# An attention recurrence with an MLP behind it: all 4630 entries of the order relisted

## The chip, the cores and the metric

The kernel runs on one core of one Trainium2 chip. A core has a matrix engine (TensorE, called PE in the profile, with its weight loads as PEld), a vector engine (VectorE, DVE), a scalar engine (ScalarE, ACT), a general engine (GpSimd, POOL) and an engine that here only issues DMAs (SyncE, SP). Each engine takes its own instructions in the order in which the program lists them, and waits at an instruction until what it needs is there. The metric is the device time of one execution in microseconds; less is better.

## What is computed

The first part is a linear attention with a state, 4 batches times 8 heads, 768 steps, 40 dimensions a head:

```python
for t in range(S):
    kt, vt, rt = (k[:, :, t], v[:, :, t], r[:, :, t])
    wt, at, bt = (w[:, :, t], a[:, :, t], b[:, :, t])
    y[:, :, t] = np.einsum('bhd,bhde->bhe', rt, state)
    Sa = np.einsum('bhde,bhe->bhd', state, at)
    state_decay = state * wt[:, :, None, :] - np.einsum('bhd,bhe->bhde', Sa, bt)
    state = state_decay + np.einsum('bhd,bhe->bhde', vt, kt)
```

Its result y, as a matrix x of 3072 tokens by 320, goes through an MLP with 2048 hidden columns:

```python
h = x @ w_in
sp = np.maximum(h, 0.0) + np.log1p(np.exp(-np.abs(h)))
g = h * erf(sp)
return (g @ w_out).astype(np.float32)
```

The weights w_in and w_out come in float64; all else is float32.

## The kernel before

**Staging.** The recurrence is cut into chunks of 32 steps. Four chunks are one segment, and there are 12 segments: two groups of batches, six segments each, and so 48 chunks one after the other, since the state MT is passed from each to the next. The MLP takes the 256 tokens of a finished segment at a time (128 steps of two batches). So the MLP of segment q lies beside the recurrence of the segments behind q, and the first MLP product can only start when the four chunks of segment 0 are through.

**Preparing a segment** has three steps that don't need the state. `prep` loads w, checks it on ACT (L447) and forms running products of it with scans on DVE (L439 and L443, two instructions each, a reciprocal L449 between them). `aphase` runs once for each chunk: it loads k, b and a, scales them on DVE (L472 makes Ab, L477 makes bk), multiplies them on PE (L482, the A product, in bank pA), masks the result on DVE (L489, two instructions), stores a part of it to DRAM, and transposes bk on PE (L500, also in pA). `tphase` runs once for a segment: it reads the parts back as Ti, inverts small triangular blocks by a recursion of 14 steps of two small DVE instructions (L529 and L530), stores the result to DRAM (TD), reads it back in another layout (Tb), transposes it on DVE (L538), and forms the rest of the inverses by two groups of small products on PE (L547, the W group and the DAD group, 64 products each, which the profile counts twice, as 128), with a copy between them and a sum (L554) behind.

**The chain of a chunk** (`chain`) is what passes the state on: copies of MT into Zm, product Z (L593), copy zt, product U (L602), copy Us, transpositions (L618, L627), product PQ (L636) and its mask on DVE (L639, into Vu), product MY (L647, L651), and then two DVE instructions that both read the bank my: L654 adds to MT, and L658 makes the output y in Pr. Behind the last chunk of a segment four transfers store y to DRAM.

**The weights** are unpacked on DVE from the words of the float64 numbers, by three instructions for each 512 columns (L737, L738, L739); those of w_in also need two split operations on PE (L754, L755) and copies of the low part (wlo). All this lies in the first 100 us.

**The MLP.** `load_x` reads y back and splits it into xh and xl. A layer-1 operation (`mm1`, L823) is eight products that split float32 into parts; two of them fill a bank ph of 128 x 512. There are 192 such operations. A copy moves ph to h (L375 when ACT does it, L377 when DVE does). `unit` takes four such blocks through six activations on ACT (L831) and two instructions on DVE (L856, L857). `post` finishes a block with L868 and L869 on DVE and four layer-2 operations on PE (L878); there are 384 of those.

**What sets the order.** `Plan.add` collects 4630 operations with what they read and write. `schedule` then gives each operation its engine by one letter of the table `ENGINES` (P for PE, A for ACT, V for DVE, G for POOL, S for SP), and `emission` writes the operations out in the sequence of the table `ORDER`, which is a list of the numbers 0 to 4629. The place in that list is all that decides what stands behind what on an engine:

```python
for i in order:
    o = N.P.ops[i]
    N.cur = i
    o["fn"](o["eng"])
```

Waits between engines follow from what the operations read and write. SP issues all the transfers, in the order of the list too. `start` also adds 190 dummy products on PE (`warm`, L422), whose result nothing reads; the list puts them where PE would else be idle, and all stand ahead of the second layer-1 block.

Of the kernel before, what the change touches and what calls it, by code (L numbers as in the profile page):

```python
# [1008 lines left out]
```

## Time and profile before

| what | value |
|---|---|
| time, median of 3 runs | 762.17 us (760.15 to 765.23) |
| span of the profiled execution | 754.8 us |
| PE busy | 722.7 us (96%) |
| DVE busy | 643.1 us (85%) |
| ACT busy | 573.3 us (76%) |
| POOL busy | 5.6 us (1%) |
| mean granted TensorE clock | 0.991 of full speed |
| DMA, mean over the span | 125 GB/s |
| largest PE groups: layer 2 (L878), layer 1 (L823, five forms) | 265.2 us, 376.2 us |

The span is the time from the first to the last instruction of one profiled execution; the device time of the runs also has what lies around it. Busy times are those of one engine, and an average over the whole span: the kernel has a start in which the MLP can't run yet, a long middle, and a short end, and these have to be looked at apart. The dummy products count as busy time of PE.

### The profile page before, as it was taken

How to read it: one execution, taken by the hardware profiler on the slowest of the kernel's cores; microseconds unless marked ns; L12 is line 12 of the kernel's file. 1: busy time of each engine (PE TensorE's matmuls, PEld its weight loads, DVE VectorE, ACT ScalarE, POOL GpSimd, SP SyncE). 2: the span in 40 equal slices, each digit the busy share in tenths (PEclk: the TensorE clock that was granted, in tenths of full speed). 3: DMA queues.
4: the chain of work that ended last, by engine and by line, in shares of the span. 5: the costliest groups of instructions: out<-in, count | busy, mean ns of one | idle time of the engine just before them, and what ended most of it. 6: DMA issues, size and time to landing. Idle time of an engine off the chain costs nothing.

```text
span 754.8 us, 32087 instructions
## 1 busy us (share of the span) xinstructions
PE 722.7 (96%) x13807; PEld 570.4 (76%) x13807; DVE 643.1 (85%) x1461; ACT 573.3 (76%) x1122; POOL 5.6 (1%) x15
## 2 busy tenths in 40 slices
PE   9968899789999999999999999999999999999996
PEld 3645558668778778878878888887888787888874
DVE  8887878889879899998889899998997898878774
ACT  3322544987988998888898897898988888776992
POOL 2000000000000000000000000000000000000000
PEclk9988999999999999999999999999999999999999
DMA  8687566655564655555545556546545444312000
GB/s 255 175 256 197 142 160 153 144 124 122 129 147 121 131 140 126 118 125 126 131 126 136 132 134 139 130 104 138 140 103 115 124 112 92 104 41 61 21 17 22
DMA packets 165616, 94.63 MB, mean 125 GB/s; under 512 B 115452, under 2 KB 148988, under 8 KB 165468
## 3 DMA queue, kind: packets, MB, share of 16 engines
q1 hardware_dynamic: 165468, 92.51, 50.1%
q8 instruction: 110, 1.80, 1.1%
q14 instruction: 38, 0.31, 0.1%
HBM read 73.48 MB, written 14.16 MB: 116 GB/s over the span
## 4 chain that ended last, share of the span: by engine, by line
PE 83%; ACT 5%; DVE 5%; DMA 3%; issue 2%; SPq 1%; DVEq 0%
PE po L878 29%; PE ph L823 22%; PE my L647 4%; PE ph L422 4%; PE pA L547 4%; PE pQ L636 4%; PE pA L482 3%; PE my L602 2%; PE my L593 2%; PE pA L500 2%; PE pQ L618 2%; PE my L651 2%; SPq L381 1%; PE pQ L627 1%; ACT l L831 1%
## 5 line engine op out<-in xcount | busy, mean ns | idle before, releaser
L878 PE MATMUL po<-wo,h 128*128 128x320 f32 x768 | 265.2, 454 | 1.1 <-DVE h L869 1.1
L878 PEld LDWEIGHTS po<-wo,h 128*128 128x128 f32 x768 | 125.5, 189 | 30.5 <-DVE h L869 1.9
L831 ACT ACTIVATE l<-l 128x512 f32<-128x512 f32 x192 | 111.0, 624 | 8.3 <-DVE nd L856 7.5
L823 PE MATMUL ph<-xh,wih 128*128 128x256 f32 x384 | 113.8, 378 | 0.0
L823 PEld LDWEIGHTS ph<-xh,wih 128*128 128x128 f32 x384 | 69.5, 190 | 24.1 <-issue 0.3
L823 PE MATMUL ph<-xh,wil 128*128 128x256 f32 x384 | 77.2, 282 | 0.7 <-issue 0.7
L823 PE MATMUL ph<-xl,wih 128*128 128x256 f32 x384 | 76.9, 282 | 0.0
L856 DVE TENSOR_TENSOR nd<-l,r 128x512 f32<-128x512 f32 x96 | 64.3, 687 | 9.6 <-ACT r L831 8.4
L868 DVE TENSOR_TENSOR l<-l,r 128x512 f32<-128x512 f32 x96 | 64.5, 682 | 1.2 <-ACT l L831 0.4
L869 DVE SCALAR_TENSOR_TENSOR h<-l,h 128x512 f32<-128x512 f32 x96 | 64.6, 684 | 0.5
L857 DVE SCALAR_TENSOR_TENSOR r<-nd,r 128x512 f32<-128x512 f32 x96 | 64.2, 683 | 0.2
L831 ACT ACTIVATE l<-h 128x512 f32<-128x512 f32 x96 | 57.6, 627 | 4.2 <-DVE h L377 3.1
L823 PEld LDWEIGHTS ph<-xh,wil 128*128 128x128 f32 x384 | 59.5, 190 | 0.7 <-issue 0.7
L375 ACT COPY h<-ph 128x512 f32<-128x512 f32 x84 | 48.9, 583 | 14.2 <-PE ph L823 13.4
L823 PEld LDWEIGHTS ph<-xl,wih 128*128 128x128 f32 x384 | 59.2, 189 | 0.0
L831 ACT ACTIVATE r<-r 128x512 f32<-128x512 f32 x96 | 55.3, 623 | 0.4
L831 ACT ACTIVATE r<-l 128x512 f32<-128x512 f32 x96 | 54.9, 621 | 0.3
L422 PE MATMUL ph<-d 104*128 104x512 bf16 x190 | 53.3, 401 | 1.6 <-DVE d L392 1.6
L823 PE MATMUL ph<-xl,wir 128*128 128x256 f32 x192 | 54.2, 282 | 0.0
L823 PE MATMUL ph<-xh,wir 128*128 128x256 f32 x192 | 54.1, 282 | 0.0
L375 ACT COPY Zm<-MT 40x320 f32<-40x320 f32 x62 | 28.3, 457 | 28.7 <-DVE MT L654 24.1
L489 DVE TENSOR_TENSOR Zs<-pA,tri 64x256 f32<-64x256 f32 x96 | 40.6, 423 | 11.1 <-PE pA L482 6.0
(142 smaller groups left out, 1346.4 us busy)
## 6 DMA issues: line engine op xcount, KB each, us to landing
bk<-in_kba_e SPq DMA_DIRECT2D x46, 416.0 KB
vt<-in_rv_e SPq DMA_DIRECT2D x96, 120.0 KB
wo<-in_moe_w_in SPq DMA_DIRECT2D x10, 512.0 KB
h<-in_moe_w_out SPq DMA_DIRECT2D x10, 512.0 KB
Pr<-in_w_e SPq DMA_DIRECT2D x12, 419.7 KB
Rt<-in_r_e SPq DMA_DIRECT2D x48, 104.0 KB
Vu<-in_v_x SPq DMA_DIRECT2D x96, 40.0 KB
Zm<-in_v_s SPq DMA_DIRECT2D x48, 80.0 KB
```

The costliest lines, as they stand in the source:

```text
L375: self.nc.scalar.copy(o, i)
L422: P.add("warm", "PE", lambda e: nc.tensor.matmul(s.ph[1], s.d1[:, :128], s.d1[:, :512], start=True, stop=True), ["d1"], ["phw"], -1e3, 0.22)
L489: P.add("Am", "DVE", lambda e, x=x, xs=xs: nc.vector.tensor_tensor(out=zx[64:128, x], in0=pz[xs], in1=s.tri[xs, None, :].to_broadcast([64, ...
L547: nc.tensor.matmul(pw[js, i, ts], l[js, i], r[js, i, ts], start=True, stop=True)
L636: nc.tensor.matmul(pq[i % 2 * 64:i % 2 * 64 + 64, i // 4, i // 2 % 2], vr[:, 256 + n_ * 64:320 + n_ * 64], vr.rearrange("p (a x) -> p a x" ...
L823: nc.tensor.matmul(ph[:, j * 256:j * 256 + 256], a[:k, fs], b[:k], start=(m == 0), stop=(m == 7))
L831: self.P.add(name, "ACT", lambda e: nc.scalar.activation(out=o, in_=i, **kw), rd, wr + ["act"], pr, 0.62)
L856: P.add("nd", [("DVE", 0.69)], lambda e, r=r, l=l, nd=nd: s.eng(e).tensor_tensor(out=nd, in0=l, in1=r, op=ALU.mult), [("l", il), ("r", ir) ...
L857: P.add("rho", "DVE", lambda e, r=r, nd=nd: nc.vector.scalar_tensor_tensor(out=r, in0=nd, scalar=2 * C4, in1=r, op0=ALU.add, op1=ALU.mult) ...
L868: P.add("E", [("DVE", 0.69)], lambda e: s.eng(e).tensor_tensor(out=l, in0=l, in1=r, op=ALU.mult), [("r", ir)], [("l", il)], pr)
L869: P.add("G", "DVE", lambda e: nc.vector.scalar_tensor_tensor(out=h, in0=l, scalar=-1.0, in1=h, op0=ALU.add, op1=ALU.mult), [("l", il)], [( ...
L878: nc.tensor.matmul(po, h[:, bs], s.wo[:, f], start=(f == 0), stop=(f == 15))
```

## The change

The tables `ORDER` and `ENGINES` are replaced. No other line differs: the same 4630 operations, with the same reads and writes. The new table is written in more lines, so every line behind it has a number that is 30 higher (L489 becomes L519, L823 becomes L853). In `ENGINES`, DVE goes from 1421 operations to 1443, ACT from 1109 to 1086, SP from 822 to 826, POOL from 11 to 8; PE keeps its 1267. The first line of the table as it was and as it is (the dummies have the numbers 27 to 216):

```diff
 ORDER = tuple(int(x) for x in """
-6 10 2 3 27 28 29 30 31 32 33 34 35 36 37 38 39 40 41 42 43 44 45 46 47 48 49 50 51 52 53 54 55 56 57 58 59 60 61 62 25 63 64 65 66 67 15 23 518 68 69 70 71 72 73 74 75 76 77 78 79
...
+2 3 23 6 17 14 16 7 4 15 11 8 19 26 10 21 20 518 5 27 28 29 30 31 32 33 34 35 36 37 38 39 40 41 42 43 44 45 46 47 48 49 50 51 52 53 54 55 56 57 58 59
...
```

Three places show what the lists do. A row is a line, an operation, its output and its inputs, and the shape; numbers behind a name are those of its buffer.

**DVE, the first microseconds, from the scans of segment 0 to the first Ab.** In the names wo and h are here the raw words of the weights, Wt and Pr the running products. Before:

```order
L738 SCALAR_TENSOR_TENSOR r_139<-wo,r_139 128x512
L739 SCALAR_TENSOR_TENSOR l_132<-wo,r_139 128x512
L737 TENSOR_SCALAR r_140<-wo 128x512
L377 COPY Zm_77<-MT 40x8x40
L738 SCALAR_TENSOR_TENSOR r_142<-wo,r_142 128x512
L449 RECIPROCAL d_115<-Wt_86 104x8
L443 SCALAR_TENSOR_TENSOR Pr_87<-Pr_87,d_115 104x516 x2
L444 COPY Pr_87<-Wt_86 104x8
L737 TENSOR_SCALAR r_139<-wo 128x512
L738 SCALAR_TENSOR_TENSOR r_139<-wo,r_139 128x512
L739 SCALAR_TENSOR_TENSOR l_136<-wo,r_139 128x512
L472 TENSOR_TENSOR Ab_76<-bk_99,Pr_87 104x512
```

Now:

```order
L469 SCALAR_TENSOR_TENSOR Wt_86<-Pr_87,d_114 104x516
L469 SCALAR_TENSOR_TENSOR Wt_86<-Pr_87,d_114 104x517
L479 RECIPROCAL d_115<-Wt_86 104x8
L473 SCALAR_TENSOR_TENSOR Pr_87<-Pr_87,d_115 104x516 x2
L474 COPY Pr_87<-Wt_86 104x8
L502 TENSOR_TENSOR Ab_76<-bk_99,Pr_87 104x512
L507 TENSOR_TENSOR bk_99<-bk_99,Wt_86 104x512
L407 COPY Zm_77<-MT 40x8x40
L767 TENSOR_SCALAR r_139<-wo 128x512
L767 TENSOR_SCALAR r_140<-wo 128x512
L768 SCALAR_TENSOR_TENSOR r_140<-wo,r_140 128x512
```

The scans, Ab and bk of the first chunk now stand at the front, and the unpacking of the weights behind them. The scan instruction is listed as SCALAR_TENSOR_TENSOR here; the trace calls it TENSOR_TENSOR_SCAN.

**PE, the W and DAD groups of segment 2.** po and wo are the bank and the weights of layer 2, my and pQ banks of the chain, pA the bank that W, DAD and A share. Before:

```order
L618 MATMUL pQ<-ident,MT 104x104 x4
L593 MATMUL my<-Zm_77,Zs_68 32x40 x16
L878 MATMUL po_165<-wo,h 128x320
L547 MATMUL pA<-T_106,Ap 32x16 x64
L878 MATMUL po_164<-wo,h 128x320 x2
L547 MATMUL pA<-Tb_83,W_104 32x16 x64
L878 MATMUL po_165<-wo,h 128x320
L482 MATMUL pA<-Ab_76,bk_99 64x2x32 x8
L602 MATMUL my<-zt_110,Tb_83 32x40 x16
```

Now:

```order
L577 MATMUL pA<-T_106,Ap 32x16 x16
L908 MATMUL po_164<-wo,h 128x320
L908 MATMUL po_165<-wo,h 128x320
L648 MATMUL pQ<-ident,MT 104x104 x4
L908 MATMUL po_165<-wo,h 128x320 x2
L577 MATMUL pA<-T_106,Ap 32x16 x48
L623 MATMUL my<-Zm_77,Zs_68 32x40 x16
L908 MATMUL po_165<-wo,h 128x320
L908 MATMUL po_164<-wo,h 128x320 x2
L908 MATMUL po_165<-wo,h 128x320
L577 MATMUL pA<-Tb_83,W_104 32x16 x64
L908 MATMUL po_164<-wo,h 128x320
```

Between the two groups of 64 there were two layer-2 products, and now there are a Z product and four layer-2 products; the first group is in two pieces.

**DVE, the end of segment 0's last chunk.** r, wo and h belong to the unpacking of the weights, vt, Vu, MT and Pr to the chain; the second L658 and the L654 beside it are the last chunk's. Before:

```order
L529 TENSOR_TENSOR tmp_107<-Ti 128x14
L530 TENSOR_TENSOR Ti<-Ti,tmp_107 128x14
L738 SCALAR_TENSOR_TENSOR r_139<-h,r_139 128x512
L658 TENSOR_TENSOR Pr_87<-my,Pr_87 104x8x32
L737 TENSOR_SCALAR r_141<-h 128x512
L472 TENSOR_TENSOR Ab_76<-bk_99,Pr_89 104x512
L639 TENSOR_TENSOR Vu_79<-pQ,tri 128x8x32
L477 TENSOR_TENSOR bk_99<-bk_99,Wt_86 104x512
L739 SCALAR_TENSOR_TENSOR wo<-h,r_139 128x512
L654 TENSOR_TENSOR MT<-MT,my 104x4x2x40
L658 TENSOR_TENSOR Pr_87<-my,Pr_87 104x8x32
L584 TENSOR_TENSOR MT<-MT,Pr_88 104x4x2x40
```

Now:

```order
L559 TENSOR_TENSOR tmp_107<-Ti 128x14
L560 TENSOR_TENSOR Ti<-Ti,tmp_107 128x14
L407 COPY vt_109<-pQ 104x8x32
L642 COPY Vu_79<-Us_85 32x4x40
L669 TENSOR_TENSOR Vu_79<-pQ,tri 128x8x32
L688 TENSOR_TENSOR Pr_87<-my,Pr_87 104x8x32
L507 TENSOR_TENSOR bk_99<-bk_99,Wt_86 104x512
L502 TENSOR_TENSOR Ab_76<-bk_99,Pr_89 104x512
L688 TENSOR_TENSOR Pr_87<-my,Pr_87 104x8x32
L684 TENSOR_TENSOR MT<-MT,my 104x4x2x40
L767 TENSOR_SCALAR r_141<-h 128x512
L614 TENSOR_TENSOR MT<-MT,Pr_88 104x4x2x40
```

L639 (now L669) has come ahead of the L472 (now L502) of the next segment, two small copies that ACT did stand ahead of it on DVE, and the last L658 (now L688) stands ahead of the L654 (now L684) of the same chunk.

## Rows read from the trace of the kernel before

**Rows 1.** Windows: stretch, length, busy of PE, PEld, DVE, ACT, POOL, PEclk, DMA, GB/s.
```profile
0.00:61.00 61.00, 51.07 (x292) 29.80 (x293) 50.65 (x110) 17.82 (x40) 5.62 (x15) 0.92 0.81 223
61.00:115.80 54.80, 49.51 (x1341) 31.02 (x1340) 43.09 (x103) 22.27 (x59) 0.00 (x0) 0.99 0.64 164
115.80:250.00 134.20, 126.33 (x2766) 105.97 (x2768) 116.83 (x277) 111.83 (x227) 0.00 (x0) 1.00 0.57 136
250.00:700.00 450.00, 447.77 (x9171) 366.14 (x9171) 397.23 (x916) 381.17 (x734) 0.00 (x0) 1.00 0.50 118
700.00:754.80 54.80, 48.01 (x248) 37.48 (x246) 35.28 (x59) 40.25 (x64) 0.00 (x0) 0.97 0.04 14
```

**Rows 2.** Windows of line L422 alone: stretch, length, PE, PEld, PEclk, DMA, GB/s.
```profile
0.00:116.00 116.00, 52.91 (x189) 18.09 (x189) 0.96 0.73 196
```

**Rows 3.** Timeline of PE: start us, length us, engine, line, out<-in, count [idle before, releaser].
```profile
1.62 21.34 PE L422 MATMUL ph<-d 104*128 104x512 bf16 x85 [1.62 <-DVE d L392]
23.97 0.69 PE L482 MATMUL pA<-Ab,bk 104*64 104x64 f32 x16
...
69.36 0.57 PE L500 MATMUL pA<-ident,bk 104*128 104x104 f32 x4 [0.47 <-DVE Zs L489]
...
115.83 0.48 PE L823 MATMUL ph<-xh,wih 128*128 128x256 f32 x2
```

**Rows 4.** Timeline of DVE, the same columns.
```profile
12.84 2.36 DVE L443 TENSOR_TENSOR_SCAN Pr<-Pr,d 104x516 f32<-104x516 f32 x2
...
19.37 0.69 DVE L477 TENSOR_TENSOR bk<-bk,Wt 104x512 f32<-104x512 f32 x1
24.76 0.86 DVE L489 TENSOR_TENSOR Zs<-pA,tri 64x256 f32<-64x256 f32 x2 [2.29 <-issue]
...
36.12 0.88 DVE L489 TENSOR_TENSOR Zs<-pA,tri 64x256 f32<-64x256 f32 x2 [0.38 <-issue]
...
43.63 0.17 DVE L529 TENSOR_TENSOR tmp<-Ti 128x14 f32<-128x14 f32 x1
...
50.21 0.19 DVE L530 TENSOR_TENSOR Ti<-Ti,tmp 128x14 f32<-128x14 f32 x1
...
53.34 1.29 DVE L739 SCALAR_TENSOR_TENSOR l<-wo,r 128x512 int32<-128x512 int32 x2
...
60.95 0.71 DVE L538 STREAM_TRANSPOSE T<-Tb 128x512 f32<-128x512 f32 x1 [1.02 <-DMA Tb<-TD]
...
101.11 0.69 DVE L472 TENSOR_TENSOR Ab<-bk,Pr 104x512 f32<-104x512 f32 x1 [1.32 <-DMA Zs<-Ab]
...
103.35 0.49 DVE L654 TENSOR_TENSOR MT<-MT,my 104x320 f32<-104x320 f32 x1
```

**Rows 5.** The chain that ended last, in order of time: start us, length us, what.
```profile
22.96 0.43 PE po L754 x2
...
51.02 4.67 DMA TD<-Ti
...
56.45 4.38 DMA Tb<-TD
...
163.44 1.30 issue
...
215.26 1.33 issue
...
655.37 0.73 PE po L878 x2
...
720.40 0.54 PE po L878 x2
```

**Rows 6.** Groups by line: engine, operation, shape, count | busy us, mean ns | idle before.
```profile
L375 ACT COPY h<-ph 128x512 f32<-128x512 f32 x84 | 48.9, 583 | 14.2 <-PE ph L823 13.4
L377 DVE COPY h<-ph 128x512 f32<-128x512 f32 x12 | 8.1, 685 | 5.6 <-PE ph L823 4.4 <-PE po L878 1.2
```

**Rows 7.** Timeline of ACT, the columns of rows 3.
```profile
4.93 1.06 ACT L447 ACTIVATE Pr<-Pr 104x1024 f32<-104x1024 f32 x1 [0.97 <-DMA Pr<-in_w_e]
```

More of the change, by code (lines that the diff above doesn't have):

```diff
@@ new lines @@
+VVVVVSSSSVPPPPAPPPPVSVVVAPVPASVVVAPVPASVVVAPAPVSVVVAPAPVSVVVAPAPASVVVAPAPASVVVAPAPASVVVAPAPASVVVAAAPAAPAASVVVAAAPVAPAASVVVSVVVSVVVSVVVSVVVSVVVSVVVSVVV
+SVVVSVVVSAVVAVSVSSVPVVSSPVSVSSVPVVSSPVSVSSVPVVSSPASVSSVPVVSSPASSSSSSVVPAPAVVAAPAPAPVPVVSSSSSSAAPAPAAAAVPAPAPVPVVSSSSSSVAPAPAAAAAPVPAPVPVVSSSSSSAAPAPAV
+AAAPAPVPVPVVSSSSSSSSAAVVVVVVVVVVVVVVVVVVVVVVVVVVVVSSSSVPPPPAPPPPVSAVSAVSSAVPPAAPPAAPPVAPPVAAAAAAAAAAAAAAAVVVVVVVVAAAAAPPAAPPAAPPVAVVPPPPPPAAVVPPPPVVPP
+PPVVPPPPSAVVAVSVSSVPVVSSPASVSSVPVVSSPASVSSVPVVSSPVSVSSVPVVSSPASSSSSSVAVPAPAAVAVPAPAPVPVVSSSSSSVAPAPASAAAPAPVPVPVVSSSSSSVVPAPASAASPVPAPVPVVSSSSSSAAPAPA
@@ new lines @@
+VAASPVPVPVPVVSSSSSSSSAAVVVVVVVVVVVVVVVVVVVVVVVVVVVVSSSSVPPPPVPPPPVSAVSVVSSAVAAAAAAAAAAAAAAVVVVVVVVAAAAAPPAAPPAAPPAAVVPPPPPPAAVVPPPPVVPPPPVVPPPPASASAAA
+AAAAAAAAAAAVVVVVVVVAAAAAPPAAPPAAPPAAVVPPPPPPAAVVPPPPVVPPPPVVPPPPSAVVVVSVSSVPVVSSPASVSSVPVVSSPASVSSVPVVSSPASVSSVPVVSSPVSSSSSSVVVPAPAAAAVPAPAPVPVVSSSSSS
+AAPAPAAVSAPAPAPVPVVSSSSSSVAPAPAASVAPAPVPVPVVSSSSSSAAPAPVAVAAPAPVPVPVVSSSSSSSSAAVVVVVVVVVVVVVVVVVVVVVVVVVVVVSSSSVPPPPAPPPPVSAVSAVSSVVAAAAAAAAAAAAAAVVVV
+VVVVAAAAAPPAAPPAAPPAAVVPPPPPPAAVVPPPPVVPPPPVVPPPPASASAAAAAAAAAAAAAAVVVVVVVVAAAAAPPAAPPAAPPAAVVPPPPPPAAVVPPPPVVPPPPVVPPPPSAVVVVSVSSVPVVSSPASVSSVPVVSSPA
@@ new lines @@
+SVSSVPVVSSPASVSSVPVVSSPASSSSSSVVAPAPAVSVVPVPAPVPVVSSSSSSVAPAPAASAAPVPAPVPVVSSSSSSAAPAPASSSVPAPAPVPVVSSSSSSVAPAPAVAVVPAPAPVPVVSSSSSSSSAAVVVVVVVVVVVVVVV
+VVVVVVVVVVVVVSSSSVPPPPVPPPPVSVVSVVSSVVAAAAAAAAAAAAAAVVVVVVVVAAAAAPPAAPPAAPPAAVVPPPPPPAAVVPPPPVVPPPPVVPPPPASVSAAAAAAAAAAAAAAVVVVVVVVAAAAAPPAAPPAAPPAAVV
+PPPPPPAAVVPPPPVVPPPPVVPPPPSAVVAVSVSSVPVVSSPASVSSVPVVSSPASVSSVPVVSSPASVSSVPVVSSPASSSSSSVAAPVPVSAVVPAPVPVPVVSSSSSSAAPAPASASAPAPAPVPVVSSSSSSAAPAPAASAVPAP
+VPVPVVSSSSSSAVPAPVAVSVPAPVPVPVVSSSSSSSSAAVVVVVVVVVVVVVVVVVVVVVVVVVVVVSSSSVPPPPVPPPPVSVVSAVSSVVAAAAAAAAAAAAAAVVVVVVVVAAAAAPPAAPPAAPPAAVVPPPPPPAAVVPPPPV
@@ new lines @@
+VPPPPVVPPPPASVSAAAAAAAAAAAAAAVVVVVVVVAAAAAPPAAPPVAPPAAVVPPPPPPAAVVPPPPVVPPPPVVPPPPSAVVVVSVSSVPVVSSPASVSSVPVVSSPASVSSVPVVSSPASVSSVPVVSSPASSSSSSVAAPVPAA
+ASVPAPVPVPVVSSSSSSVAPAPAASVAPAPAPVPVVSSSSSSAAPAPASSAAPAPVPVPVVSSSSSSAAPAPVAAVAPAPAPVPVVSSSSSSSSAAVVVVVVVVVVVVVVVVVVVVVVVVVVVVSSSSVPPPPAPPPPVSAVSAVSSAV
+AAAAAAAAAAAAAAVVVVVVVVAAAAAPPAAPPAAPPAAVVPPPPPPAAVVPPPPVVPPPPVVPPPPASASAAAAAAAAAAAAAAVVVVVVVVAAAAAPPAAPPAAPPVAVVPPPPPPAAVVPPPPVVPPPPVVPPPPSAVVAVSVSSVP
+VVSSPASVSSVPVVSSPASVSSVPVVSSPASVSSVPVVSSPVSSSSSSVAVPVPVVVVVPVPAPVPVVSSSSSSAAPAPVAVASPAPAPVPVVSSSSSSAAPAPASSVSPAPAPVPVVSSSSSSAAPVPVAASAPAPAPVPVVSSSSSSS
```

41 lines of the change are left out of this document (15 added, 26 removed), and 269 rows, old and new, of the table ORDER.

## The prediction

> **What bounds the kernel now.** I read the busy times by stage first [rows 1]. The columns to compare are the length of a stretch and PE's busy time in it. From 250 to 700 us PE is idle for 450.00 - 447.77 = 2.2 us in all, although DVE (88%) and ACT (85%) are nearly as full. A new order of the same operations can hardly save anything there. From 115.8 to 250 us PE is idle for 7.9 us. From 700 us to the end it is idle for 6.8 us, most of it behind the last product, which no order hides. Up to 115.8 us PE looks 87% busy, but 52.9 us of that are dummy matmuls of L422 [rows 2]. So the kernel has two halves. Up to the first layer-1 matmul at 115.83 us [rows 3] nothing but a chain of latencies counts. Behind it PE works through a fixed list. The end moves with the moment at which that list can start, and with the 7.9 us of holes just behind it.
>
> Next I followed the chain of latencies on PE [rows 3], on DVE [rows 4] and through the transfers [rows 5]: first A product at 23.97 us, last masked A block (L489) from 36.12 to 37.00, recursion (L529, L530) from 43.63 to 50.40, two transfers through DRAM (TD, Tb), transposition L538 at 60.95, then four chunks that each end with L654 (the last at 103.35), the store and reload of x, and the first matmul of the MLP at 115.83. The reader is to see that the first A waited behind 85 dummies and the split operation after them. Its last input, L477 at 19.37, was done at about 20.0, and DVE then stood idle for 2.29 us ahead of its first L489.
>
> **The change, part by part.** No operation is added or taken away; the tables decide order and engine alone. Counted over both tables, DVE gains 22 operations and ACT loses 23. By their durations in the profile that is about 9 us moved from ACT to DVE, spread over the run: net eight copies of ph (583 ns on ACT, 685 on DVE [rows 6]), six of vt, five of the output and some smaller ones.
>
> *First chunk.* Before, nine weight operations (L737, L738, L739) stand ahead of the first L472; after, none. The scans need w, which had landed when ACT checked it at 4.93 us [rows 7]. From there two scan pairs at 2.36, a reciprocal and a copy (0.4), L472 and L477 at 0.61 (two weight operations in a row take 1.29, so one more of this size costs 0.61 [rows 4]): done at 11.3 us. PE now has 38 dummies ahead of the first A instead of 86: 1.62 + 38 x 0.251 (85 took 21.34 [rows 3]) = 11.2 us. So the first A runs at 11.3 us, 12.7 earlier. Little of this is passed on, for the dummies are only moved. Between the first and the second A there are now 35 of them (8.8 us), three split operations of 0.86 (two steps of 0.43 [rows 5]) and a transposition, so the second A runs at 24.2 us; by the same count the third at 27.4, the fourth at 31.2, and the last L489 ends at 32.4 instead of 37.0: **4.6 us** earlier.
>
> *Recursion.* Behind the last L489 DVE has 7.9 us of work before the recursion (four weight operations, two scan pairs, a copy) where it took 6.6. Start at 40.3 instead of 43.63, end at 47.1 instead of 50.40: **3.3 us**.
>
> *The two transfers.* From the recursion's end to L538 it took 10.55 us, of which TD 4.67 and Tb 4.38 [rows 5], with the DMA engines at 0.81 over the first 61 us [rows 1]. The bulk loads are the same in either order, and five of the w_out loads are issued ahead of Tb in both. The gain is 3.3 us if the trip takes as long as it did. If it is shorter, DVE's own list between recursion and transposition (8.0 us of it) is the bound, and the gain is 5.8. I take **4.0**, near the row, since the loads are only pressed into a shorter time. The Trainium skill (DMA: Bandwidth & Descriptors, section Latency and other measured facts) gives a DMA a fixed cost of about 2 us, mostly HBM latency that rises with load; with two trips of about that, DVE's list would be the bound and the whole sum 753.9 us. The trace's 4.67 and 4.38 speak against it while bulk loads run beside.
>
> *To the first U.* Before, a transposition (L500) that waited 0.47 us for DVE [rows 3] stood ahead of the first U (L602); now it stands behind. Against that, six split operations stand ahead of the W products instead of partly between them. **0.8 us** gained (0 to 1.5).
>
> *The chunks.* Before, L639 of the last chunk stood behind an L472 that waited 1.32 us for a transfer [rows 4] and took 0.61; now L639 comes first, but behind two small copies (0.6). In the chunk before, 0.9 us of small copies and a recursion step are put ahead of L639. Net **0.6 us** gained (between 0.9 lost and 1.8 gained). In the last chunk L658, which the store of x waits for, is put ahead of L654: **0.4 us**.
>
> So the first layer-1 matmul comes 4.0 + 0.8 + 0.6 + 0.4 = 5.8 us earlier, at 110.0 us (bounds 2.4 and 9.5).
>
> *Behind it.* PE has the same 192 layer-1 and 384 layer-2 operations. A layer-2 operation takes 0.54 us behind a full-width one and 0.73 behind a group of narrow tiles [rows 5], so grouping could save time. But the steps from narrow to full width, counted in PE's two lists, are 176 in each. That is worth nothing. What does change is the spacing of the W and DAD groups (L547; each product is short, and 128 of them stand in a group). Before, 1.3 us of other work lies between them in segment 2 and 2.4 in segment 3, and PE stood still inside the second group for 1.30 and 1.33 us with nothing to wait for that the profile shows [rows 5]. After, 2.8 and 5.0 us lie between; in segment 5 it shrinks from 3.3 to 1.2. I take **1.5 us** gained, between 0 and the 2.6 of these two rows.
>
> The price: between the first layer-1 and the first layer-2 operation DVE's list grows by 2.7 us (two L856, one L857, one L868 and one copy of ph more, some small copies fewer). DVE is 87% busy from 115.8 to 250 us [rows 1], so some of it shows: **0.8 us** lost (0 to 2.7). ACT's list there keeps its length.
>
> Sum: 5.8 + 1.5 - 0.8 = 6.5 us. The profiled execution has a span of 754.8 us; the median of the runs is 762.17, so about 7.3 us lie around the span if that execution was a middling one. Predicted: 748.3 us of span, **755.7 us** of time.
>
> **Rivals.** *The start gives more.* The transfers land early, the chunks close up, the stalls go: at most 9.5 + 2.6 = 12.1 us. Half-way from the forecast to that is 9.5 us, a time of 752.7. For it: by the lists alone, with no transfer late, the first layer-1 matmul could come at 107.6. Against it: some thirty waits must all be met.
>
> *The gain is eaten.* TD and Tb are held by the bulk loads, the holes behind 115.8 us stay and DVE's longer list shows: 2.4 - 0.8 = 1.6 us gained, time about 760.6. For it: the DMA engines are at 0.81 already. A page's rule goes the same way for one term: by the Trainium skill (Runtime: NRT & Kernel Launch, section Instruction fetch mechanics) the refill of an engine's instruction memory is mostly hidden, so the stalls at L547 would have another cause, which spacing need not cure; that alone would give 757.2. The two rows without a releaser show a stall, not its cause.
>
> *Slower.* DVE becomes what PE waits for between 250 and 700 us, where it is 88% busy and gains some 6 us of moved copies. A chunk there is about 13 us long (48 chunks in some 620 us), so 34 fall into that stretch. In each, the chain MT, Zm, Z, zt, U, Us, Vu, MY must fit while PE has other work. If PE runs dry for 0.5 us in each, that is 17 us less the 6.5 gained: 772.7 us. It decides (over 1% slower) from (7.6 + 6.5) / 34 = 0.41 us in a chunk. Against it: idle time there is 2.2 / 34 = 0.07 us in a chunk.
>
> **How the numbers follow.** The forecast (754 to 759 us) 0.46, more 0.27, eaten (759 to 763) 0.20, slower 0.07. One per cent, about what a measurement of this kernel can tell from no change, is 7.6 us: faster is below 754.5, slower above 769.8. About 0.09 of the forecast's 0.46 lies below 754.5. So faster 0.27 + 0.09 = 0.36, slower 0.07, and the rest, 0.57, the same. The range 749.5 to 762.5 leaves out the slower case and the ends of the others.
>
> **What would show it.** In the profile after (its lines are 30 higher): first A product (L512) at 11 to 12 us; last L519 ended by 33; recursion (L559) from about 40; transposition L568 at 55 to 58; first L853 at 107 to 112; PE idle for 2 to 4 us between 250 and 700; no stall of over 1 us without a releaser inside L577 in segments 2 and 3. A first L853 after 113 would refute the steps of the start. PE idle for more than 8 us between 250 and 700 would refute that the middle is full in either order.

## The result, and the profile after

| | before | after |
|---|---|---|
| time, median of 20 runs | 761.98 us | 769.36 us |
| ratio to before | | 1.0101 (95%: 1.0081 to 1.0121) |
| span of the profiled execution | 754.8 us | 769.7 us |
| PE busy | 722.7 us | 725.9 us |
| DVE busy, ACT busy | 643.1, 573.3 us | 655.4, 565.9 us |
| first layer-1 matmul in that execution | 115.83 us | 118.80 us |

The change made the kernel 7.4 us slower, where 6.5 us faster was forecast; that is just the one per cent that the text took as the bound of what can be told. The two profiles are 14.9 us apart and so show twice the difference of the medians. The reason: the profiled execution of the changed kernel took 771.53 us with a span of 769.7, so 1.8 us lie around a span, not 7.3 as the prediction worked out. The execution of before on record took about 754.8 + 1.8 = 756.6 us, one of the quickest of its 20 (756.35 is the least). A second profile of the kernel before (below) has a span of 762.8 us and is used beside the first. An execution more than 1.5% above the quickest of its kernel stands outside the ratios: so one of 1345.58 us among the 20 after, three of the twelve of old_to_250 below, and four of the twelve of start_old, its profiled one (773.08 us) among them.

The windows of the changed kernel answer to [rows 1]. The columns are again stretch, length, busy time of PE, PEld, DVE, ACT and POOL, granted clock, DMA share, GB/s:

```profile
0.00:61.00 61.00, 50.13 (x425) 30.68 (x425) 55.67 (x115) 19.76 (x45) 4.44 (x12) 0.94 0.87 235
61.00:115.80 54.80, 48.38 (x1168) 30.36 (x1169) 38.12 (x95) 19.94 (x55) 0.00 (x0) 0.91 0.61 153
115.80:250.00 134.20, 126.44 (x2695) 103.59 (x2693) 117.11 (x269) 103.46 (x209) 0.00 (x0) 0.97 0.53 129
250.00:400.00 150.00, 145.26 (x3060) 117.60 (x3059) 133.33 (x316) 125.61 (x240) 0.00 (x0) 1.00 0.54 126
400.00:550.00 150.00, 145.34 (x3011) 117.97 (x3010) 132.98 (x311) 122.44 (x240) 0.00 (x0) 1.00 0.52 123
550.00:700.00 150.00, 149.32 (x3077) 122.45 (x3076) 128.74 (x300) 125.86 (x236) 0.00 (x0) 1.00 0.42 101
```

Two things are to be seen. Between 250 and 550 us PE is now idle for 4.7 + 4.7 = 9.4 us; from 250 to 700 us it was 2.2 in all. And the granted clock of the stretch before the MLP has fallen from 0.99 to 0.91. Closer, from the same view of the changed kernel:

```profile
105.00:110.00 5.00, 3.98 (x170) 2.58 (x170) 4.08 (x8) 0.34 (x2) 0.00 (x0) 1.00 0.68 157
110.00:115.00 5.00, 4.15 (x148) 2.64 (x148) 1.21 (x3) 2.08 (x6) 0.00 (x0) 0.73 0.48 121
115.00:120.00 5.00, 5.00 (x51) 3.11 (x49) 3.05 (x9) 1.00 (x3) 0.00 (x0) 0.58 0.77 232
```

So PE is near the lower of its two levels, 1.2 GHz, just where the MLP is to begin; the first profile of before has 1.00 in each of these three stretches. It is the new start that brings this: all eleven profiles that have it, those of the experiments below among them, show the half clock for 7 to 14 us somewhere between 107 and 125 us, and none of the six with the old start does. What it costs in the total is another matter, as start_new will show.

**Lost time of PE.** To compare many profiles, PE's lost time is counted the same way in each: for every operation on PE behind the first layer-1 matmul, the time from the end of the operation ahead of it to its own end, less the smallest such time that the same pair of kinds of operations shows in any of the profiles. It holds idle time and low clock. Means, by the layer-1 operations as milestones (the old list from the two profiles of before and start_new below; the new one from the profiles after, new_again, new_bk_later, new_dummies, new_dummies_store and start_old):

| stretch, by layer-1 operation | about, us | old list | new list |
|---|---|---|---|
| 1 to 24 | 119 to 190 | 8.1 us | 8.8 us |
| 25 to 40 | 190 to 250 | 2.1 | 3.6 |
| 41 to 82 | 250 to 395 | 3.5 | 6.0 |
| 83 to 114 | 395 to 510 | 2.9 | 6.6 |
| 115 to 180 | 510 to 715 | 3.1 | 3.5 |
| 181 to the end | 715 to 765 | 1.4 | 3.2 |
| sum | | 21.1 | 31.6 |

The list itself, by the smallest times, is 1.4 us cheaper (610.0 against 611.4). What was lost is in the waits, and its two densest places are 395 to 510 us and the tail. The nine executions behind the table are not all middling ones: the six of the new list took 10.9 us longer in the mean than the three of the old one (772.5 against 761.6), not 7.4, so the table shows more than the change costs.

### The profile page after: what moved, and what is told of

Read it like the earlier page. It is cut to its first block, busy times and chain, and to the rows that moved or that the text cites. A ratio compares the mean times of both kernels' runs of the same rounds, so it can differ in the third digit from the quotient of the medians.

```text
span 769.7 us, 32101 instructions
## 1 busy us (share of the span) xinstructions
PE 725.9 (94%) x13807; PEld 570.4 (74%) x13807; DVE 655.4 (85%) x1483; ACT 565.9 (74%) x1099; POOL 4.4 (1%) x12
## 4 chain that ended last, share of the span: by engine, by line
PE 63%; DVE 15%; DMA 11%; SPq 4%; issue 4%; ACT 2%; DVEq 0%; ACTq 0%
PE po L908 21%; PE ph L853 17%; SPq L411 4%; PE pA L577 3%; PE my L677 3%; PE ph L452 3%; PE pA L512 3%; PE pQ L666 2%; DMA bk<-in_kba_e 2%; PE my L632 2%; PE my L623 2%; PE pA L530 2%; DVE Wt L469 2%; PE pQ L648 2%; DMA Tb<-TD 2%
## 5 line engine op out<-in xcount | busy, mean ns | idle before, releaser
L908 PE MATMUL po<-wo,h 128*128 128x320 f32 x768 | 246.3, 444 | 1.6 <-DVE ob L407 1.5
L908 PEld LDWEIGHTS po<-wo,h 128*128 128x128 f32 x768 | 131.3, 190 | 38.0 <-DVE ob L407 2.0
L853 PE MATMUL ph<-xh,wih 128*128 128x256 f32 x384 | 100.5, 343 | 0.8 <-DVE h L407 0.8
L853 PE MATMUL ph<-xl,wih 128*128 128x256 f32 x384 | 77.2, 283 | 0.0
L853 PE MATMUL ph<-xh,wil 128*128 128x256 f32 x384 | 77.1, 282 | 0.0
L853 PEld LDWEIGHTS ph<-xh,wih 128*128 128x128 f32 x384 | 63.4, 190 | 13.7 <-DVE h L407 1.0
L899 DVE SCALAR_TENSOR_TENSOR h<-l,h 128x512 f32<-128x512 f32 x96 | 65.3, 685 | 0.9
L898 DVE TENSOR_TENSOR l<-l,r 128x512 f32<-128x512 f32 x96 | 64.9, 683 | 0.9
L853 PEld LDWEIGHTS ph<-xh,wil 128*128 128x128 f32 x384 | 59.7, 191 | 0.0
L853 PEld LDWEIGHTS ph<-xl,wih 128*128 128x128 f32 x384 | 59.5, 190 | 0.0
L452 PE MATMUL ph<-d 104*128 104x512 bf16 x190 | 54.9, 418 | 1.6 <-DVE d L422 1.6
L853 PE MATMUL ph<-xl,wir 128*128 128x256 f32 x192 | 54.4, 283 | 0.0
L853 PE MATMUL ph<-xh,wir 128*128 128x256 f32 x192 | 54.1, 282 | 0.0
L677 PE MATMUL my<-Vu,sg 64*40 64x72 f32 x1536 | 47.5, 232 | 4.4 <-DMA Vu<-Us 1.7
L405 ACT COPY h<-ph 128x512 f32<-128x512 f32 x76 | 43.6, 579 | 10.8 <-PE ph L853 10.7
L519 DVE TENSOR_TENSOR Zs<-pA,tri 64x256 f32<-64x256 f32 x96 | 40.6, 423 | 11.5 <-PE pA L512 8.2
```

The lines of the kernel that those rows point to most:

```text
L405: self.nc.scalar.copy(o, i)
L452: P.add("warm", "PE", lambda e: nc.tensor.matmul(s.ph[1], s.d1[:, :128], s.d1[:, :512], start=True, stop=True), ["d1"], ["phw"], -1e3, 0.22)
L519: P.add("Am", "DVE", lambda e, x=x, xs=xs: nc.vector.tensor_tensor(out=zx[64:128, x], in0=pz[xs], in1=s.tri[xs, None, :].to_broadcast([64, ...
L677: nc.tensor.matmul(my[h * 64:h * 64 + 40, x, j], sg[xs, j, h], vu[xs, j // 2 * 2 + h, j % 2], start=True, stop=False)
L853: nc.tensor.matmul(ph[:, j * 256:j * 256 + 256], a[:k, fs], b[:k], start=(m == 0), stop=(m == 7))
L898: P.add("E", [("DVE", 0.69)], lambda e: s.eng(e).tensor_tensor(out=l, in0=l, in1=r, op=ALU.mult), [("r", ir)], [("l", il)], pr)
```

## The experiments

In the diffs, OLD and NEW are the two lists; `upto(X, n)` is what list X has ahead of its layer-1 operation n + 1, and `rest(X)` is X without what is already placed. Every operation keeps the engine of the list that places it. Ratios are to the kernel before on the same chip. In the rows shown of these kernels, line numbers lie 3 lower than in the changed kernel (L499 is its L502).

### The start and the rest apart

```diff
-ORDER = NEW
+ORDER = upto(NEW, 0) + rest(OLD)
```

> The operations that the new order lists ahead of the first layer-1 matmul, in that order and on those engines; all others as before. Theory 1 (the new start itself costs: its first layer-1 matmul came at 118.8 us where it was 115.8, and what PE gets late it ends late): 3 us slower, ratio 1.004, first layer-1 matmul near 119. Theory 2 (the loss is in the operations behind, which stand too close to DVE, ACT and transfers): ratio 1.000, whatever the first matmul does. Theory 3 (the slow clock that the new start leaves behind and the holes after it are the whole loss): ratio 1.010.

Measured: 0.9989 (0.9962 to 1.0016). Theory 2: the new start costs nothing, and brings nothing, its half clock ahead of the MLP included. Its first layer-1 matmul came at 122.3 us.

```diff
-ORDER = NEW
+ORDER = upto(OLD, 0) + rest(NEW)
```

> The mirror image: the old order up to the first layer-1 matmul, the new one for all behind it. Theory 1: the rest of the loss is left, some 4 us, ratio 1.006, first layer-1 matmul near 116. Theory 2: all of the loss is left, ratio 1.010. Theory 3: ratio 1.000.

Measured: 1.0032 (0.9989 to 1.0076). By time this decides little: the 1.010 of theory 2 lies outside, but 1.000 and 1.006 both lie inside. The first matmul came at 122.0 us, with the very list that had it at 115.8 in the profile on record, so this moment is a draw of several us in either order. PE's lost time behind it is 31.3 us, that of the new list; that speaks for theory 2, in the profile of one of its longer executions.

```diff
-ORDER = NEW
+ORDER = upto(OLD, 40) + rest(NEW)
```

> The old order up to the 41st layer-1 operation (243 us in the old trace), the new one behind it. In the two profiles 8.4 of the 14.9 us are there by this operation and 6.5 come later; the medians differ by 7.4. If the new order of the middle is itself looser on PE: ratio 1.003 to 1.005, with PE idle for some 8 us between 250 and 550 us. If the later part of the difference belongs to one slow and one quick execution: ratio 1.000, PE idle for 2 to 3 us there.

Measured: 1.0013 (0.9979 to 1.0048), too near to 1 to separate the two cases by time. In its profile PE loses 26.6 us, of which 5.4 in operations 83 to 114 and 3.2 in the tail, as the new list does.

### The two kernels again

> The changed kernel as it is, for a second profile and for its time beside the repairs below. If the holes of the first profile belong to the order and not to one execution, the same places show them: two of 1.0 and 1.5 us behind 730 us, PE's clock near 0.5 of full speed between 110 and 120 us, and DVE and ACT together some 15 to 18 us in front of instructions that wait for a transfer between 116 and 700 us (5 us in the kernel before). If they belong to the execution, they are elsewhere. Ratio to before 1.006 to 1.010.

Measured: 1.0085 (1.0054 to 1.0116), first matmul at 120.2 us. The clock is down again ahead of the MLP, 0.87 from 110 to 115 us and 0.50 from 115 to 120, and between 250 and 700 us PE is idle for 6.3 us, where the first profile has 10.1. The places are the same: the two holes of the tail are there to the hundredth (1.06 and 1.74 us), and DVE and ACT stand 13.7 us in front of transfers between 130 and 700 us. The holes belong to the order.

> The kernel before as it is, for a second profile. The profile on record (span 754.8 us, time some 756.6) was among its quickest executions. If its quick start (first layer-1 matmul at 115.8 us) was a draw, it is at 117 to 122 here, with the same holes behind it as in the first profile; if it belongs to the order, 115 to 116.5.

The time was 764.59 us, the first matmul at 122.9 us, lost time 21.6 us behind it (20.2 in the first profile), DVE and ACT 6.6 us in front of transfers. The quick start on record was a draw, and the places behind it repeat.

### What takes the gain of the start

Milestones of the start, in us. The old start was seen in six profiles (also with old_to_250, old_400_tail, start_old, old_users_early), the new one in nine (after, new_again, start_new, new_dummies, new_old_tail, patient, patient_tail, new_400_tail, new_tight):

| end of, or begin of | old: range, mean | new: range, mean |
|---|---|---|
| last L489 of segment 0, end | 35.8 to 37.0, 36.1 | 33.7 to 34.1, 33.8 |
| recursion, begin | 42.4 to 43.6, 42.9 | 41.4 to 41.8, 41.5 |
| L538, begin | 59.0 to 61.0, 60.2 | 57.3 to 58.2, 57.7 |
| first U, begin | 68.9 to 72.0, 70.3 | 66.9 to 69.7, 67.8 |
| last MY of segment 0, end | 103.3 to 109.4, 106.2 | 101.1 to 105.5, 103.1 |
| last xl, end | 115.3 to 122.3, 118.6 | 116.8 to 120.6, 118.9 |
| first layer-1 matmul | 115.8 to 122.9, 119.2 | 118.8 to 122.3, 120.8 |

The chain does run 3 us ahead down to the last chunk. It is between MY and the first matmul that 4.7 us are lost. DVE and SP in the changed kernel, by their timelines (start, length, instruction, [idle before, releaser]):

```profile
102.07 0.69 DVE L507 TENSOR_TENSOR bk<-bk,Wt 104x512 f32<-104x512 f32 x1 [2.23 <-DMA bk<-in_kba_e]
102.68 0.68 DVE L502 TENSOR_TENSOR Ab<-bk,Pr 104x512 f32<-104x512 f32 x1
103.28 0.42 DVE L688 TENSOR_TENSOR Pr<-my,Pr 104x256 f32<-104x256 f32 x1
```

```profile
102.93 1.75 SPq L411 DMA_DIRECT2D Tb<-TD  x2
104.78 1.81 SPq L411 DMA_DIRECT2D xd<-Pr  x4
109.31 2.59 SPq L411 DMA_DIRECT2D xr<-xd  x4
```

MY ended at 101.1, but L688, which the store waits for, stood behind L507, which waited 2.23 us for its load. Then the stores stood on SP behind the Tb loads. PE meanwhile, in the same kernel:

```profile
101.01 2.76 PE L452 MATMUL ph<-d 104*128 104x512 bf16 x12
105.37 0.62 PE L623 MATMUL my<-Zm,Zs 96*32 96x40 f32 x32 [1.60 <-ACT Zm L405]
...
114.70 2.31 PE L452 MATMUL ph<-d 104*128 104x512 bf16 x5
116.81 0.90 PE L530 MATMUL pA<-ident,bk 104*128 104x104 f32 x4
...
118.80 0.76 PE L853 MATMUL ph<-xh,wih 128*128 128x256 f32 x2
```

Five dummies take 2.31 us, 0.46 each, where the 12 of 101.01 us took 0.23 each, and they stand ahead of the first layer-1 matmul, whose last operand (L837) was there at 116.8. Three kernels took these apart:

```diff
-DVE: ... L507, L502, L688, L684, L767, L614, Zm
+DVE: ... L688, L684, L767, L614, Zm, L507, L502
```

> The changed kernel with two DVE operations (the scalings L507 and L502 of segment 1's last chunk, of which the first waited 2.23 us for its load) moved behind L688, L684, L614 and the copy Zm at the end of segment 0's last chunk. Theory 1: the store of x starts 2 to 3 us earlier, PE has less idle time ahead of the first layer-1 matmul, and the time falls by as much: ratio to the kernel before 1.006. Rival: the reload of x or the clock takes it back, ratio 1.010.

Measured: 1.0053 (1.0029 to 1.0078), and 1.0085 (1.0054 to 1.0116) for the kernel without the edit; the intervals overlap. In its profile y was ready at 104.6 us, but the stores were issued at 108.05, behind Tb loads that waited for TD until 106.61; first matmul at 123.15. The wait moved from DVE to SP. The time is near theory 1's 1.006, and the rival's 1.010 is outside the interval; the profile, of its slowest execution (776.38 us), shows what the rival said.

```diff
-PE: MY, 12 dummies, Z ... 2 dummies, W ... DAD, 2 dummies, A, 5 dummies, bT, dummy, U, dummy, L853
+PE: MY, 18 dummies, Z ... 5 dummies, W ... DAD, A, bT, U, L853
```

> The changed kernel with nine dummy products (of those that stand between the DAD group of segment 1 and the first layer-1 matmul) moved ahead: six ahead of the Z product of segment 1's first chunk, where PE stood for 1.6 us, three ahead of the W group, where it stood for 0.65. Theory A (PE's own list at the low clock is what delays the first layer-1 matmul, since its operands were there at 116.8 and it began at 118.8): the granted clock stays above 0.8 between 110 and 120 us, and the first matmul follows its last operand (L837) by less than 0.8 us: 2 to 3 us earlier. Rival (the store, the reload and DVE delay it): the first matmul comes no earlier than 118 and the dummies only change places.

Measured: 1.0068 (1.0025 to 1.0110). The first matmul now followed its last operand by 0.1 us, but that operand came later (119.0), and the clock fell all the same:

```profile
115.00:120.00 5.00, 3.60 (x56) 3.08 (x57) 3.97 (x10) 1.16 (x5) 0.00 (x0) 0.50 0.78 199
```

So the half that theory A said of the operands came true, the one on the clock did not, and the time is the rival's.

```diff
-SP: Tb, Tb, xd, xd, xd, xd
+SP: xd, xd, xd, xd, Tb, Tb
```

> The same, and the four stores of x moved ahead of the two Tb loads on SP, and L507 and L502 of segment 1's last chunk behind L688, L684 and L614. Theory B (the stores stand on SP behind the Tb loads, which wait for TD: 104.8, 106.5 and 108.1 us in three profiles, where y was ready 1.1, 2.5 and 3.4 us before): the stores are issued within 1 us of the last L688, and the first layer-1 matmul comes 2 us earlier than with the dummies alone, near 114 to 115. Rival: the Tb loads come later by the same 2 us, the W and DAD groups with them, and the first matmul, which stands behind them on PE, gains nothing.

Measured: 1.0114 (1.0078 to 1.0150). The stores were issued at 105.29 us, within 0.1 us of the end of y's last multiplication, and the Tb loads at 106.98. The W group, which stood at 107.6 in the first profile, came at 111.5, and the first matmul at 121.2: the rival. The two chains, x and Tb, share SP and meet again on PE, and what one gains the other loses. None of the three repairs brought the first matmul forward (123.15, 119.1 and 121.2 us, against 118.8 and 120.2 of the changed kernel), so how the 4.7 us divide among the load, the stores and the dummies is not shown.

### Transfers, and who stands behind them

Between 130 and 700 us DVE and ACT stand 3.8 to 6.6 us in front of transfers in three profiles of the old list, and 13.7 to 19.2 in six of the new one. An example from the changed kernel (DVE, then ACT, then PE):

```profile
446.50 0.69 DVE L502 TENSOR_TENSOR Ab<-bk,Pr 104x512 f32<-104x512 f32 x1 [1.17 <-DMA Zs<-Ab]
447.22 0.49 DVE L407 COPY sg<-pA 128x320 f32<-128x320 f32 x1
447.63 0.41 DVE L407 COPY vt<-pQ 104x256 f32<-104x256 f32 x1
```

```profile
450.21 0.40 ACT L405 CAST xh<-xr 128x256 fp32r<-128x256 f32 x1 [2.94 <-DMA xr<-xd]
450.52 0.62 ACT L861 ACTIVATE r<-l 128x512 f32<-128x512 f32 x1
451.17 0.32 ACT L642 COPY Vu<-Us 32x160 f32<-32x160 f32 x1
```

```profile
448.10 0.73 PE L666 MATMUL pQ<-vt 104*64 104x64 f32 x16 [0.86 <-DVE vt L407]
...
451.83 0.39 PE L677 MATMUL my<-Vu,sg 64*40 64x72 f32 x5 [1.25 <-DMA Vu<-Us]
```

The copies to vt and Vu, which PE waits for, stand behind instructions that wait for a transfer. The last row names a DMA as releaser; the ACT copy to Vu at 451.17 us ends 0.3 us ahead of it and fits better. Three kernels tested whether this is the cause:

```diff
-ACT: xh, ln2, Vu, ln2, ln2, tbl
+ACT: ln2, Vu, ln2, ln2, tbl, xh
...
```

> The changed kernel with ten operations of ACT and DVE moved behind the next one to four operations of their engine: those that in six profiles with the new list of the middle stood waiting for a transfer (T0 of four segments, an xh, three ab, two bk; 0.6 to 2.9 us each, about 11 us together of the 14 to 19 that DVE and ACT wait for transfers between 130 and 700 us; before it is 4 to 5). Theory (these waits hold up the chain's copies behind them, and PE runs dry): the waits fall to 6 to 9 us, PE's holes between 116 and 700 us fall from 26 to 29 us to 21 to 24, and the time by some 5 us, ratio 1.003. Rival (the waits lie in slack of these engines, and the holes have other causes): the waits fall and the holes stay, ratio 1.008.

Measured: 1.0127 (1.0080 to 1.0174). The waits fell, to 7.6 us, and the lost time did not, 32.4 us. At four places it went as the theory said: an A product from 0.95 to 0.07 us, a transposition from 1.3 to 0, a PQ from 0.93 to 0, a W group from 0.88 to 0. But others opened. Here is one, on DVE and then on PE in this kernel:

```profile
454.76 0.69 DVE L499 TENSOR_TENSOR Ab<-bk,Pr 104x512 f32<-104x512 f32 x1 [2.33 <-DMA Zs<-Ab]
...
456.58 0.68 DVE L504 TENSOR_TENSOR bk<-bk,Wt 104x512 f32<-104x512 f32 x1
```

```profile
457.36 0.69 PE L509 MATMUL pA<-Ab,bk 104*64 104x64 f32 x16 [1.98 <-ACT l L858]
```

One of the ten, a bk, had gone behind an Ab, which now had to wait itself, and the A product behind both came 2 us late. The theory falls as a repair: ten waits fewer are not ten holes fewer.

```diff
-ORDER = NEW with the ten moves
+ORDER = upto(that, 180) + rest(OLD)
```

> The same ten moves, and the order and engines of before behind the 181st layer-1 operation, which took 1.9 us of holes out of the tail. By the theory the two repairs add up: 7 us off, ratio 1.000 to 1.001. Rival: 1.005, the tail alone.

Measured: 1.0074 (1.0041 to 1.0106), lost time 29.3 us: the tail's part came off, 1.5 us, operations 83 to 114 still lose 6.7 us, and the theory's 1.000 to 1.001 lies outside the interval, the rival's 1.005 inside.

```diff
-DVE, ACT: ..., 1.4 us of other work, ab | bk | xh | T0
+DVE, ACT: ..., ab | bk | xh | T0, 1.4 us of other work
```

> The kernel before with the opposite done to it: between 130 and 700 us every ab, bk, xh and T0 (115 operations that use what a transfer brings) stands some 1.4 us of its engine's work earlier; nothing else moves. Theory: DVE and ACT wait 12 to 25 us for transfers there, where it was 4 to 5, PE's holes grow by 5 to 10 us, ratio 1.007 to 1.013. Rival: the waits grow and PE's holes don't, ratio 1.000.

Measured: 1.0263 (1.0197 to 1.0328), more than the theory's range. DVE and ACT waited 35.0 us for transfers (6.6 in the second profile of before), and PE lost 49.2 us where it lost 21.6. So users put too close to their transfers do open holes on PE, about as long as the waits. That this is possible is shown; that it is what the new list suffers from is not, by the ten moves.

### Two places

```diff
-ORDER = NEW
+ORDER = upto(NEW, 180) + rest(OLD)
```

> The changed kernel up to its 181st layer-1 operation (of 192), the order and engines of before for all behind it. If the two holes of the tail (1.05 us ahead of a layer-1 product that waited for a copy of ph on DVE, 1.73 us at a layer-2 product that waited for a copy of the output on DVE) come from the new list of the tail: both are gone, PE's excess behind 700 us is 1.5 us where it was 3.6, and the time falls by 2 us, 0.3% (less than the interval of the ratio can prove). If they come from what stands further ahead, they stay.

Measured: 1.0049 (1.0023 to 1.0075), a median of 768.35 us against 771.34. Lost time in the tail is 1.7 us instead of 3.2, as expected: of its two holes the first is gone, and the second fell from 1.73 to 0.91 us. They were these, on PE in the changed kernel:

```profile
732.63 0.50 PE L853 MATMUL ph<-xh,wih 128*128 128x256 f32 x2 [0.79 <-DVE h L407]
...
745.71 17.64 PE L908 MATMUL po<-wo,h 128*128 128x320 f32 x64 [1.47 <-DVE ob L407]
```

The first stands directly behind the layer-1 operation that fills the same bank, and so waits for the copy of that bank (0.69 us on DVE) with nothing between; the old list has three layer-2 products there. The second waits for the copy of the finished output, which DVE takes up only behind two L898 and two L899; the old list has it ahead of the last L869.

```diff
-ORDER = NEW
+ORDER = upto(NEW, 80) + [i in upto(OLD, 114)] + [i in upto(NEW, 180)] + rest(OLD)
```

> The changed kernel with the list of before in two windows: from the 81st to the 114th layer-1 operation (some 395 to 510 us) and from the 181st to the end. By the count of PE's holes the new list has 3.5 us more than the old one between 400 and 500 us and 2.2 more behind 700 (medians over the profiles). If these places carry most of the loss: both differences are gone from the profile, the ratio is 1.001 to 1.003 where the changed kernel has 1.0085. Rival (holes only move: what is taken out in one place comes back at the next wait, as in the kernel with the ten moves): PE's holes stay near 30 us and the ratio above 1.006.

Measured: 1.0004 (0.9973 to 1.0036). The time fits the theory: its 1.001 to 1.003 lie in the interval, the rival's 1.006 does not. Lost time in operations 83 to 114 is 4.0 us instead of 6.6 (2.9 in the old list), in the tail 1.7 instead of 3.2, and DVE and ACT stand 9.6 us in front of transfers. The whole of the lost time, though, is 29.7 us, near the rival's figure; the profile is of its slowest execution (769.11 us, where the median is 765.32).

```diff
-ORDER = OLD
+ORDER = upto(OLD, 80) + [i in upto(NEW, 114)] + [i in upto(OLD, 180)] + rest(NEW)
```

> The mirror image: the kernel before with the new list in the same two windows. If these places carry the loss: PE's holes 25 to 27 us where the kernel before has 20 to 21.7, ratio 1.005 to 1.007. Rival: 20 to 22 us and 1.000 to 1.002.

Measured: 1.0053 (1.0019 to 1.0087). Lost time is 4.8 us in the first window, 3.2 in the tail, and 27.1 in all, in a profile of its quickest execution (765.35 us); DVE and ACT stand 10.1 us in front of transfers. So the two places swap most of the loss by time: new with the old places is the kernel before, within 0.4%, its interval apart from that of new_again, and old with the new places is half a per cent slower. About half of the additional waits for transfers moved with them. Two things keep this from being the whole: old_to_250 has both places from the new list and came to 1.0013 (0.9979 to 1.0048), which overlaps with 1.0053 and with 1; and the lost time of new_400_tail did not come down as its time did. That a new start is not needed for a loss, these kernels show; that the two places alone carry it, they do not show to the end.

### The groups of short products

```diff
-PE: 128 W, Z, 4 layer-2 products, 128 DAD
+PE: 128 W, Z, 128 DAD, 4 layer-2 products
```

> The changed kernel with the layer-2 products that it puts between the W and the DAD group of segments 2 and 3 (four and seven) moved behind the DAD group. The prediction's step on the groups of short products: with them apart the stalls inside the second group, 1.5 to 1.8 us in segment 2 and 0.4 to 1.6 in segment 3 with the old list, are 0.1 to 0.7 and 0.1 to 0.9. If the spacing did that, they are back here: over 1.2 us inside the DAD group of segment 2, over 0.8 in segment 3, with nothing that the profile shows as releaser. If not, PE waits only ahead of the group, for the copy between the two groups.

One execution: 783.5 us. In segment 2 the stall is back; PE, by its timeline in this kernel:

```profile
168.19 1.18 PE L574 MATMUL pA<-T,Ap 32*32 32x16 f32 x96
...
170.43 1.01 PE L574 MATMUL pA<-Tb,W 32*32 32x16 f32 x98 [0.63 <-DVE W L404]
173.01 0.62 PE L574 MATMUL pA<-Tb,W 32*32 32x16 f32 x30 [1.57 <-issue]
...
225.70 1.91 PE L574 MATMUL pA<-Tb,W 32*32 32x16 f32 x128 [1.65 <-ACT W L402]
```

After 98 of 128 products PE stood for 1.57 us without a releaser, as in the old list [rows 5]. In segment 3 PE waited 1.65 us ahead of the group, for the copy W, and ran all 128 without a stop; there the expected stall did not come.

What PE waits for at such a stall is in the traces, in a queue that the account of DMA lists apart. In the page of the changed kernel it is

```profile
q8 instruction: 110, 1.80, 1.0%
```

that is, 110 packets of 16 KiB, which bring PE its instructions. In the 17 profiles there are 70 stalls of more than 0.3 us inside a W or DAD group, and all 70 end 1.2 to 1.7 us behind the end of such a packet and stand at the same place of PE's own sequence of instructions, the 193rd or 194th when its matmuls, weight loads and semaphore instructions are counted modulo 256. Here the packet took from 170.49 to 171.58 us and the stall ended at 173.01; of the two stalls of before in [rows 5] the packets ended at 163.43 and 215.04 us and the stalls at 164.74 and 216.59. So PE uses up instructions faster in a run of short products than they are brought. In segment 3 the packet had ended at 223.18 us, and the wait for the copy W had given it the time. Distance from the group before helps for this reason, whether it is work or a wait. The time, 12 us over the median of the changed kernel, is larger than these rows; PE's lost time grew from about 31 to 42 us in this execution, and where the rest comes from was not followed up.

## Why the prediction was wrong, step by step

**First chunk.** The first A ran at 12.60 us, not 11.3. DVE's two scan pairs started at 6.16 us, behind a copy of 1.97 and a memset of 0.92, which the count left out. The second A, 24.47 for 24.2, and the fourth, 31.57 for 31.2, came as counted, since dummies and splits set them. The last L519 ended at 33.70 for 32.4, and against the mean of the old start the gain is 2.3 us, not 4.6.

**Recursion and transfers.** From the last L519 to the recursion it took 7.7 us for 7.9; it began at 41.43 (41.5 in the mean), 1.4 us earlier than the old mean, not 3.3. L568 at 57.27 is inside the 55 to 58 forecast, a gain of 2.5 for 4.0 by the means. But the prediction's other branch is what came: DVE's own list was the bound, not the trip.

```profile
56.93 0.43 DVE L767 TENSOR_SCALAR r<-h 128x512 int32<-128x512 int32 x1
57.27 0.70 DVE L568 STREAM_TRANSPOSE T<-Tb 128x512 f32<-128x512 f32 x1
```

The transposition stands there with no wait ahead of it, as in all eleven profiles with the new start, while all six with the old start wait 1.0 to 1.7 us for Tb. The list from the recursion's end took 9.3 us for the 8.0 counted, 0.58 of it a wait for weights. So of the 2.5 us, 1.4 come from the recursion and 1.1 from the trip, where 3.3 and 0.7 were forecast. The Trainium skill (DMA: Bandwidth & Descriptors, section Latency and other measured facts) would have made DVE the bound with trips of 2 us; DVE was the bound here though the trips of segment 0 took 3.3 us (TD, from 48.64) and 4.2 us (Tb, from 52.76).

**First U and chunks.** First U 2.5 us ahead, last MY 3.1, of 5.4 forecast by then. Right in mechanism, 0.57 of the size.

**The step that failed in the start** is the sentence that the first layer-1 matmul comes earlier by the sum of what is gained above it. It took the way from the last chunk to the MLP as fixed, 12.5 us as in the rows. The means are 119.2 - 106.2 = 13.0 us with the old list and 120.8 - 103.1 = 17.7 with the new. What stands in that way now: L688 behind L507, which waits for a load (2.23 us); stores behind Tb on SP (up to 3.4 us in the repairs); and dummies at half the clock. How the 4.7 us divide among them is not shown, since no repair brought the first matmul forward. In the part on the chunks the loads of bk were not looked at, though L507 stands directly ahead of L688 in the rows of the order. Even had it passed on everything, the start would have been worth 3 us.

**Behind the first layer-1 matmul.** The spacing term was right where it was made: PE's idle time in and just ahead of the W and DAD groups of segments 2 and 3 falls from 2.8 us (mean of three profiles) to 0.4 (mean of five with the new list), more than the 1.5 forecast. But in segments 5, 6 and 8 the groups of the new list have 2.8 us where the old had 0.8, so little of it is left; in operations 83 to 114 stalls of this kind make 1.5 us in the mean of the new list and 0.7 in that of the old. By the Trainium skill (Runtime: NRT & Kernel Launch, section Instruction fetch mechanics) the refill is mostly hidden. The traces agree for the most part, and not at these stalls: of some 108 blocks in the first profile of before, seven have a stall of more than 0.15 us behind the first layer-1 matmul, 4.6 us in all. There the refill is what PE waits for, so the stalls did not have another cause, and spacing does cure them. The 0.8 us for DVE's list ahead of the first layer-2 matmul came out as 0.7 (8.1 to 8.8 in the table).

**The step that cost most** is the first one: that PE is full between 250 and 700 us, so that a new order can hardly save anything there. It can't save, but it can lose, and the sum has no term for that. By the table the new list loses 6.6 us more than the old from operation 41 to 180 and 1.8 in the tail, and gives back 1.4 by its cheaper sequence. The right rival was in the prediction, at a chance of 0.07 and with a loss spread evenly over 34 chunks; it sits for the most part in a few chunks and the tail instead. The prediction's own bound for the middle, PE idle for more than 8 us between 250 and 700, was passed in the first profile, 4.74 + 4.66 + 0.68 us by the windows above; the second profile of the changed kernel, with 6.3 us, stays below it, and the three of the old list have 2.2 to 3.8.

**The time of the profile.** Taking 7.3 us for what lies around the span was wrong (1.8), and with it the reading that the profiled execution was a middling one. A slip without effect on the forecast: half way between the 6.5 us and the 12.1 of the first rival is 9.3, not 9.5.

What stays open: which feature of the list makes the holes at the two places. It is not the ten waits for transfers alone; DVE's and ACT's copies, the wait for Tb and the refill of PE's instructions all stand there, and their shares are not shown. No version was found that is faster than the kernel before by more than its runs scatter.

## To carry to other kernels

A stretch where the bounding engine is 99% busy has nothing to gain from a new order and everything to lose; it needs a term in the sum. Which feature of a list sets the size of that term stayed open here. Before a gain at the start is passed on to the end, follow it through every queue that it crosses, the DMA-issuing one above all. And take a second profile of the kernel before: one execution can be 7 us from the next in a single milestone (115.8 to 122.9 us).

## What was not expected of the hardware

- The same order of the start reached its first layer-1 matmul between 115.8 and 122.9 us in six executions.
- The granted clock fell ahead of the MLP, to the lower of its two levels, in all eleven profiles with the new start, and in none of the six with the old; in the first profile of the changed kernel (0.58 from 115 to 120 us) PE had stood idle several times between 103 and 112 us, and it fell with nine more dummies in that gap too (0.50). The new start with the rest of the old list took no longer for it (0.9989). Dummies at the low clock take 0.46 us instead of 0.23 and delay the work behind them.
- In a run of 128 short products PE can run out of instructions: stalls of up to 2.2 us end 1.2 to 1.7 us behind the end of a 16 KiB packet of the instruction queue, always at one place of each 256 instructions of PE's sequence, 70 times in 17 profiles. One such group stopped for 1.57 us after 98 of its products when the group before it had ended 1.1 us earlier, and another ran through when it began after a wait of 1.65 us.
